# Copying the P V output banks out by ScalarE before VectorE normalises them, with smaller rings and a new order

## Chip, core and metric

The kernel runs on one core of a Trainium2 chip. The time is device microseconds for one execution, the median of several runs; a profiled execution of the same program gives the trace. TensorE (PE in the profile) does matmuls into PSUM, which has eight banks of 2 KB a partition. ScalarE (ACT) and VectorE (DVE) read the banks; GpSimd (POOL) and SyncE (SP) mostly issue transfers and pass on semaphores here.

## The reference

The input x has 2048 tokens of width 448, in bf16. It is normalised over the width, and two branches read the result xn:

```
xn = layernorm(x)
q, k, v = split(xn @ wqkv)                     # 16 heads of 28
logits[s, w] = q[s] . k[s - 2 w] / sqrt(28)    # w = 0..7, positions below 0 masked
s = concat_heads(softmax(logits) @ v) @ wo     # sliding, dilated attention
g = silu(gelu(xn @ w1 + b1) @ w2 + b2)         # 448 -> 1792 -> 448
out = x + s * g
```

## The kernel before

Tokens are reordered into the even and the odd ones, so that the dilation of 2 becomes a window of 8 neighbours. There are 16 tiles of 128 tokens and four chunks of 512. For each tile the kernel computes statistics (stats, L444), the normed row xn (norm, L479), a transpose of it (by TensorE for the first four tiles, by a DMA transpose for the others, dma_T, L398), the q and k rows (qk_rows, L576; matmuls L582), transposed by DMA into qkT, and the v rows (vproj, L599; matmuls L605), stored to v_hbm and loaded again in the layout of the blocks (values, L617).

Attention runs over nine blocks of 228 tokens (224 for the fifth). For a block, spread (L632) prepares the keys, scores_of (matmuls L757) fills four banks with scores, weights_of applies the exponential on ScalarE (L766) and the mask on VectorE (L772), and values_of (matmuls L786) multiplies the weights P with the values V into two banks. P V is done for two blocks together (four banks) and for block 8 alone. In output_of, VectorE normalises each bank in four steps: a 32x32 block transpose that brings the row sums into reach (L795), a reciprocal (L799), a transpose that spreads it back (L804), and a multiply into oT (L809), after which the bank is free.

The MLP runs by chunk: ff1 (matmuls L658, gelu on ScalarE L662), ff2 (matmuls L690, and L712 for the last two tiles), the gate (L724, L736, L740, or L731 for the last four tiles), and final with wo (matmuls L856, and L864 for the last two tiles), the gated sum (L876, L878, L883) and the output's transfer (L887).

Most matmuls use 64 of the 128 rows, two at a time: pair (L521) runs two jobs a and b with the first half of the rows for one and the second half for the other, and then swaps them. Between the halves a no-operation on GpSimd (L538) waits for the first half's matmuls and releases the second half's, the hop.

The order is made by a planner when the program is built (_Plan, L56): every piece of work is a task with an engine, a cost, its dependences, a priority, and the buffers it takes and gives. The planner takes the task that can start first, and among those that can start about then the one with the highest priority (tables PRIO and LATER, with corrections for single tasks by number in NUDGE). Each engine then runs its list in that order. Buffers come from rings: p_E (exponentials, four a block), p_v (values, one a block), p_xn (normed rows), p_b (the eight banks).

Of the kernel before, what the change touches and what calls it, by code (L numbers as in the profile page):

```python
# [8 lines left out]
F32 = mybir.dt.float32  # L9
BF16 = mybir.dt.bfloat16  # L10
ALU = mybir.AluOpType
ACT = mybir.ActivationFunctionType
# [5 lines left out]
TILED = 30  # L18
BURST = 3.5
NUDGE = {  # L20
    51: -17, 100: 72, 158: 186, 160: 19, 169: -108, 170: 110, 184: -158, 227: -173, 230: -199, 398: -138,
    428: -8, 461: 105, 892: 15,
}
LAST = 352
SAME = 20
# [155 lines left out]
def kernel(  # L181
# [12 lines left out]
    nc = tc.nc  # L194
    P = 128
    S, D, H, DH, F = A_x.shape[1], 448, 16, 28, 1792
# [14 lines left out]
    NW, NK, BACK, PAD = 57, 64, 7, 16  # L211
    VIS = []
    for v in range(9):
        n = NW - 1 if v == 4 else NW
# [18 lines left out]
    def sb(name, shape, dt=BF16):  # L233
        return const.tile(shape, dt, name=name)
# [29 lines left out]
    def ring(name, n, shape, dt=BF16, fifo=False):  # L264
        return _Pool([sb(f"{name}{i}", shape, dt) for i in range(n)], fifo)

    p_xn = ring("xn", 4, [P, 512])
    p_st = ring("st", 4, [P, 6], F32)
    p_E = ring("E", 15, [P, 8 * NW], fifo=True)
    p_dt = ring("dt", 2, [P, 512], F32)  # L270
    p_rd = ring("rd", 2, [P, H], F32)
    p_y = ring("y", 2, [P, D], F32)
    p_t = ring("t", 2, [P, D], F32)
# [4 lines left out]
    late_g = [w_in[:, kt, w * D:(w + 1) * D] for kt in range(3) for w in range(3)]  # L278
    p_g.bufs = p_g.bufs + late_g
    p_h = ring("h", 28, [P, CH], fifo=True)  # L280
    p_v = ring("v", 4, [P, 4, H // 2, 32], fifo=True)
    p_k = ring("kd", 2, [P, G, 4, 2 * NK], fifo=True)
    qk_tok = [sb(f"qk_tok{i}", [P, 2, H, 32]) for i in range(4)]
    p_f = _Pool([None])
# [1 line left out]
    p_b = _Pool([psum.tile([P, 512], F32, name=f"bank{i}") for i in range(8)])  # L286


    PRIO = {
        "project": (136, 119.5, 53, -443.5,),  # L290
        "project2": (38, -0, -278, -679.5,),
        "values": (-43, -278, -332, -863,),
        "attn": (95, 33.5, 174.5, 3, 187.5, 61, 136.5, 427, 178.5,),
        "ff1": (110.5, 186, 49, 159, -18.5, 129.5, 87, 189.5, 92, 142, 185, 18, 156, 198, 89, 31.5,
            202.5, 86, 62.5, -70.5, 140, 20.5, 76.5, 126.5, -3, 181, 92, 212.5,),
        "gelu": (120.5, -49.5, 86, -3,),
        "ff2": (195, -34.5, -231.5, 114.5, 68.5, 89, 111.5, 135, 195, 180.5, 162, 104, 430, 131,
            99.5, 28.5,),
        "final": (128.5, 2, 1, -16.5, 41.5, -2, 41, 203, 110, 65.5, 194.5, 162.5, 189.5, 134, 208,
            148,),  # L300
        "norm": (131, 11, 219.5, 294, 32, 66.5, 83.5, 207.5, 87.5, 115, 14, 127, 142.5, 64, 52.5,
            80,),
        "loads": (125, 117.5, -97.5, 131, 140.5, 12.5, 4, 84,),
        "stats": (49, 32, 205.5, 205.5, 131.5, 117, 41, 114, 130, 91, 157, 32.5, 140.5, 101.5,
            153.5, 258.5,),
        "turn_x": (198, 4.5, 200, 12.5, 258.5, 205.5, 24.5, 200, 24.5, -25.5, 154, 60, 132, 183.5,
            146.5, 78.5,),
        "turn_qk": (187, 122.5, 29, 78, -20.5, -22.5, 153.5, -151, 65.5, 6.5, 138, 32, 198.5, 162,
            35, 226.5,),
        "move_v": (146, 183, -68, 180, 92.5, 154.5, 241.5, 140.5, 190,),  # L310
        "store_v": (175, 54, 86, -1.5, 139.5, 189.5, -0, 18.5, 82.5, 213, 109.5, -126, 116, 13,
            53.5, 32,),
        "spread": (92, 81.5, 89, 141, 58, 25.5, 142, 46.5, 42,),
        "copies": (187, 4, 219, 15.5, 90, 177, 88.5, 31, 29, 20.5, 182, 51, 204.5, 49.5, 24,),
    }
    LATER = {"swap": 231.5, "qk": 165, "v": 171.5, "gelu": 94, "exp": 96.5, "mask": -4417.5, "pv": 209.5, "recip": 201.5, "os": 234, "y": 195, "tanh": 106, "g": 185.5, "sg": 100.5, "o": 89.5}

    plan = _Plan()

    def buf(pool, owner, i=0):  # L320
        return pool.bufs[owner.slots[pool][i]]

    def pe(n, k=1):
        return k * (n / 2400.0 + 0.0025)

    def act(n):
        return 0.15 + n / 1130.0

    def dve(n, r=1):
        return 0.15 + n / (960.0 * r)  # L330
# [186 lines left out]
    def behind(later, earlier):  # L517
        tc.add_manual_dep(later.ins, earlier.ins.name,
                          mybir.DependencyInfo(mybir.DependencyClass.Sync, mybir.DependencyReason.DATA), reason="row tiles")

    def pair(a, b, prio, early=False, before=(range(4),), after=(range(3),), late=((),), give=()):  # L521
# [21 lines left out]
        for i, ks in enumerate(after):  # L543
            def f3(k, ks=ks, n=n, i=i):
                p, q = buf(p_b, t, 0), buf(p_b, t, 1)
                for x in together([part(b, q, kt, 0, n + m) for m, kt in enumerate(ks)], [part(a, p, kt, 1, n + m) for m, kt in enumerate(ks)])[0]:
                    if not i:
                        behind(x, held["told"])
            u = plan.add("PE", pe(a.n, len(ks)), f3, [u if i else told], prio + LATER["swap"], give=give if i + 1 == len(after) else (), tail=0.15, mode=64)
            n += len(ks)  # L550
# [25 lines left out]
    def qk_rows(t, which, prio):  # L576
# [7 lines left out]
        def evac(a, own, i):  # L584
            b = qk_tok[t % len(qk_tok)]

            def fn(k):
                copy(k.on, b[:, which, :, :DH], buf(p_b, own, i)[:, :D].rearrange("p (h c) -> p h c", h=H))
            t_row[t].append(plan.add(("ACT", "DVE"), (act(D), dve(D)), fn, [a, t_qz[t % len(qk_tok)], t_qk.get(t - len(qk_tok))],
                                     prio + LATER["qk"], give=((p_b, own, i),)))  # L590
            if len(t_row[t]) == 2:
# [60 lines left out]
    def ff1(c, mt, prio, gate):  # L652
# [7 lines left out]
        def evac(a, own, i):  # L660
            def fn(k):
                nc.scalar.activation(buf(p_h, own, i)[:], buf(p_b, own, i)[:], ACT.Gelu_apprx_tanh,  # L662
                                     bias=b1[:, mt:mt + 1])
            t_h[(c, mt)] = plan.add("ACT", 0.69, fn, [a, t_b1] + gate, prio + LATER["gelu"],
                                    give=((p_b, own, i),), table=("gelu",))
# [53 lines left out]
    def gate(t, cs, n, a, own, i, biased, prio):  # L719
        if biased:  # L720
            y, pool, at, held = own, p_b, i, ((p_b, own, i),)
        else:
            def f2(k):
                nc.vector.tensor_tensor(out=buf(p_y, k)[:, :n], in0=buf(p_b, own, i)[:, :n], in1=b2[:, cs], op=ALU.add)  # L724
            y, pool, at = plan.add("DVE", dve(n), f2, [a, t_b2], prio + LATER["y"], take=(p_y,), give=((p_b, own, i),)), p_y, 0
            held = ((p_y, y, 0),)
        after = [a, y]

        if t >= NT - TPC:
            def f5(k):  # L730
                nc.scalar.activation(buf(p_g, k)[:, :n], buf(pool, y, at)[:, :n], ACT.Silu)  # L731
            t_g[t].append(plan.add("ACT", act(n), f5, after, prio + LATER["tanh"], take=(p_g,), give=held, table=("silu",)))
            return
# [56 lines left out]
    def output_of(b, po, i, a, prio):  # L790
        q, n1 = VIS[b]
        n, m = 8 * n1, -(-8 * n1 // 32)

        def f5(k):
            nc.vector.transpose(buf(p_dt, k)[:, :32 * m], buf(p_b, po, i)[:, :32 * m])  # L795
        d = plan.add("DVE", dve(32 * m), f5, [po], prio + LATER["recip"], take=(p_dt,))

        def f6(k):
            nc.vector.reciprocal(buf(p_rd, k)[:, :m],  # L799
                                 buf(p_dt, d)[:, :32 * m].rearrange("p (b c) -> p b c", c=32)[:, :, DH])  # L800
        r = plan.add("DVE", 0.25, f6, [d], prio + LATER["recip"] + 5, take=(p_rd,))

        def f7(_):
            nc.vector.transpose(buf(p_dt, d)[:, :32 * m].rearrange("p (b c) -> p b c", c=32),  # L804
                                buf(p_rd, r)[:, :m].unsqueeze(2).to_broadcast((P, m, 32)))
        rb = plan.add("DVE", dve(32 * m), f7, [r], prio + LATER["recip"] + 10, give=((p_rd, r, 0),))

        def f8(_):
            nc.vector.tensor_tensor(out=oT[:, a::2, q:q + 4 * n1],  # L809
                                    in0=buf(p_b, po, i)[:, :n].rearrange("p (l q) -> p l q", l=2),  # L810
                                    in1=buf(p_dt, d)[:, :n].rearrange("p (l q) -> p l q", l=2), op=ALU.mult)
        o = plan.add("DVE", dve(n), f8, [rb], prio + LATER["os"], give=((p_b, po, i), (p_dt, d, 0)))
        for t in range(q // P, (q + 4 * n1 - 1) // P + 1):
            t_oT[t].append(o)

# [144 lines left out]
    def f_b1(k):  # L960
# [3 lines left out]
                    give=((p_b, b1_at, 0),))  # L964
# [84 lines left out]
```

## Time and profile before

| | |
|---|---|
| median of 3 runs | 154.95 us (154.22 to 155.2) |
| profiled execution, its time | 154.93 us |
| its span | 153.2 us |
| busy: TensorE, VectorE, ScalarE, GpSimd | 146.5, 116.9, 91.5, 20.0 us |
| granted TensorE clock | 1.00 |

The span is the time from the first to the last instruction that the profile shows; the execution's own time has some 1.7 us more around it. In the chain of work that ended last, each row is followed back to what released it, so that time on the chain is time that the end hangs on. "bank" is a PSUM bank, "xT" holds the transposed normed rows and later, under the name oT, the attention output; "POOLq" and "SPq" are the instruction queues of GpSimd and SyncE; a line number such as L658 is a line of the kernel before.

### The profile page before, as it was taken

The numbers are of one execution on the slowest core, as the hardware profiler recorded it, in microseconds if no ns is written. First come the engines' busy times: TensorE is split into PE (matmuls) and PEld (weight loads), VectorE is DVE, ScalarE is ACT, GpSimd is POOL, SyncE is SP. The second block draws the span as 40 slices with busy tenths as digits, with TensorE's granted clock in tenths as the row PEclk, the third lists the DMA queues.
The fourth block names the chain that finished last, engine by engine and source line by source line (L and its number), as shares of the span: only waits on it lengthen the run. The fifth ranks groups of instructions, "written<-read, shape, count | busy, mean of one in ns | idle before, by whom it ended". The sixth has DMA issues, their size and how long they took to land.

```text
span 153.2 us, 5216 instructions
## 1 busy us (share of the span) xinstructions
PE 146.5 (96%) x2169; PEld 82.8 (54%) x2169; DVE 116.9 (76%) x285; ACT 91.5 (60%) x159; POOL 20.0 (13%) x53
## 2 busy tenths in 40 slices
PE   7799999999999999999999979999999999999990
PEld 2454444544455556455576733454569985754460
DVE  3887950573668857996898899789998966999962
ACT  3246887557695534574689578816984666660220
POOL 6536440110660000000130000000000000000000
PEclk9999999999999999999999999999999999999999
DMA  4999969999575361271389999722010030000131
GB/s 147 309 288 327 157 119 193 282 348 241 134 173 108 68 137 23 54 137 37 132 189 225 210 159 138 202 85 73 0 53 11 4 120 6 0 4 0 35 121 30
DMA packets 38022, 19.47 MB, mean 127 GB/s; under 512 B 24887, under 2 KB 37246, under 8 KB 37998
## 3 DMA queue, kind: packets, MB, share of 16 engines
q1 hardware_dynamic: 37246, 17.58, 51.0%
q0 software_dynamic: 608, 1.44, 3.6%
q8 instruction: 17, 0.28, 0.7%
q10 hardware_dynamic: 144, 0.11, 0.2%
q14 instruction: 7, 0.06, 0.1%
HBM read 9.42 MB, written 3.94 MB: 87 GB/s over the span
## 4 chain that ended last, share of the span: by engine, by line
PE 93%; DMA 2%; DVE 2%; issue 1%; ACT 0%; POOLq 0%
PE bank L658 28%; PE bank L690 24%; PE bank L582 14%; PE bank L605 7%; PE bank L856 7%; PE bank L786 4%; PE bank L712 4%; PE bank L757 3%; DMA x_sb<-in_A_x_dram 2%; PE bank L864 1%; DVE st L446 1%; PE bank L500 1%; DVE xn L481 0%; DVE xT L336 0%; DVE sg L876 0%
## 5 line engine op out<-in xcount | busy, mean ns | idle before, releaser
L658 PE MATMUL bank<-xT,w 64*128 64x512 bf16 x392 | 44.9, 376 | 1.3 <-POOLq L538 1.0
L662 ACT ACTIVATE h<-bank,b 128x512 bf16<-128x512 f32 x56 | 34.3, 686 | 17.5 <-PE bank L658 17.5
L690 PE MATMUL bank<-w,h 64*128 64x448 bf16 x392 | 39.8, 349 | 0.0
L658 PEld LDWEIGHTS <-w 64*128 64x128 bf16 x392 | 21.7, 94 | 22.0 <-POOLq L538 2.4
L690 PEld LDWEIGHTS <-h 64*128 64x128 bf16 x392 | 20.5, 94 | 15.7 <-issue 0.3
L582 PE MATMUL bank<-w_in,xT 64*128 64x448 bf16 (+1 forms) x212 | 24.7, 349 | 0.2 <-issue 0.2
L766 ACT ACTIVATE E<-bank 128x456 bf16<-128x456 f32 (+1 forms) x36 | 17.0, 557 | 4.8 <-PE bank L757 3.6
L334 ACT CAST qk_tok<-bank 128x448 bf16<-128x448 f32 x21 | 10.8, 535 | 12.8 <-PE bank L582 9.9
L582 PEld LDWEIGHTS <-xT 64*128 64x128 bf16 (+1 forms) x212 | 11.1, 94 | 9.4 <-POOLq L538 0.6
L795 DVE STREAM_TRANSPOSE dt<-bank 128x480 f32<-128x480 f32 (+1 forms) x18 | 12.1, 671 | 3.0 <-PE bank L786 2.9
L605 PE MATMUL bank<-w_in,xT 64*128 64x448 bf16 (+1 forms) x106 | 13.8, 350 | 0.1
L336 DVE CAST qk_tok<-bank 128x448 bf16<-128x448 f32 x11 | 6.7, 624 | 8.9 <-PE bank L582 8.8
L804 DVE STREAM_TRANSPOSE dt<-rd 128x480 f32<-128x480 f32 (+1 forms) x18 | 12.1, 675 | 0.6
L856 PE MATMUL bank<-wo,xT 64*128 64x448 bf16 x112 | 12.3, 349 | 0.0
L809 DVE TENSOR_TENSOR xT<-bank,dt 128x456 bf16<-128x456 f32 (+1 forms) x18 | 11.4, 632 | 0.6
L724 DVE TENSOR_TENSOR y<-bank,b 128x448 f32<-128x448 f32 x15 | 8.7, 618 | 4.1 <-PE bank L690 4.1
L446 DVE BATCH_NORM_STATS2 st<-x_sb 128x6 f32<-128x448 bf16 x16 | 9.6, 607 | 2.6 <-DMA x_sb<-in_A_x_dram 2.6
L772 DVE TENSOR_TENSOR E<-E,m_gen 128x456 bf16<-128x456 bf16 (+1 forms) x32 | 11.2, 390 | 0.0
L481 DVE TENSOR_SCALAR xn<-x_sb,mv,rstd 128x448 bf16<-128x448 bf16 x16 | 6.3, 401 | 4.4 <-POOL rstd L469 4.3
L736 ACT ACTIVATE t<-y 128x448 f32<-128x448 f32 x12 | 6.6, 583 | 4.0 <-DVE y L724 4.0
L856 PEld LDWEIGHTS <-xT 64*128 64x128 bf16 x112 | 6.6, 94 | 4.0 <-issue 0.4
L605 PEld LDWEIGHTS <-xT 64*128 64x128 bf16 (+1 forms) x106 | 5.9, 94 | 4.3 <-DVE xT L336 0.3
(74 smaller groups left out, 136.8 us busy)
## 6 DMA issues: line engine op xcount, KB each, us to landing
v<-v_hbm SPq DMA_DIRECT2D x14, 128.0 KB, 3.1
out_dram<-o SPq DMA_DIRECT2D x15, 112.0 KB, 1.7
v_hbm<-v_tok SPq DMA_DIRECT2D x13, 128.0 KB, 3.2
w<-in_B_w_dram SPq DMA_DIRECT2D x2, 672.0 KB, 7.4
w_in<-in_A_wqkv_dram SPq DMA_DIRECT2D x3, 336.0 KB, 4.4
w<-in_B_w_dram SPq DMA_DIRECT2D x2, 448.0 KB, 5.7
x_sb<-in_A_x_dram SPq DMA_DIRECT2D x4, 224.0 KB, 5.5
w<-in_B_w_dram SPq DMA_DIRECT2D x2, 336.0 KB, 6.3
```

The source lines that it names most:

```text
L446: nc.vector.bn_stats(out=buf(p_st, k)[:], in_=x_sb[:, t, :])
L582: return nc.tensor.matmul(ps[:, :D], xnT[r, kt, cs], w, start=start, stop=stop)
L605: return nc.tensor.matmul(ps[:, :D], xnT[r, kt, k0:k0 + P], w, start=start, stop=stop)
L658: return nc.tensor.matmul(ps[:], w1[r, kt, ms], xnT[r, kt, cs], start=start, stop=stop)
L662: nc.scalar.activation(buf(p_h, own, i)[:], buf(p_b, own, i)[:], ACT.Gelu_apprx_tanh, bias=b1[:, mt:mt + 1])
L690: return nc.tensor.matmul(ps[:, :D], buf(*h_at[(c, mt)])[r, cs], w2[r, mt, :], start=start, stop=stop)
L766: nc.scalar.activation(buf(p_E, k)[:, :8 * n], buf(p_b, a, at + i)[:, :8 * n], ACT.Exp, scale=SCALE)
L772: nc.vector.tensor_tensor(out=E, in0=E, in1=m[:, :, :, :n].rearrange("p i g q -> p (i g) q"), op=ALU.mult)
L795: nc.vector.transpose(buf(p_dt, k)[:, :32 * m], buf(p_b, po, i)[:, :32 * m])
L804: nc.vector.transpose(buf(p_dt, d)[:, :32 * m].rearrange("p (b c) -> p b c", c=32), buf(p_rd, r)[:, :m].unsqueeze(2).to_broadcast((P, m, 32)))
L809: nc.vector.tensor_tensor(out=oT[:, a::2, q:q + 4 * n1], in0=buf(p_b, po, i)[:, :n].rearrange("p (l q) -> p l q", l=2), in1=buf(p_dt, d)[: ...
L856: return nc.tensor.matmul(ps[:, :D], oT[r, kt, t * P:(t + 1) * P], wo[r, kt, :], start=start, stop=stop)
```

## The change

A ScalarE copy takes each output bank of P V into one of three fp32 buffers (p_oc); the bank is free after the copy. VectorE's first transpose and its last multiply read that buffer, which is free after the multiply. To make room, the ring of exponentials goes from 15 to 12 buffers, that of values from 4 to 3 and that of normed rows from 4 to 3. All priorities and the corrections by task number are other values, so that the order on every engine is another one; the number of matmuls of each kind is the same. The first P V stands nearer to the scores before it, and the parts of the projections of chunks 2 and 3 lie between other matmuls than before.

```diff
 NUDGE = {
-    51: -17, 100: 72, 158: 186, 160: 19, 169: -108, 170: 110, 184: -158, 227: -173, 230: -199, 398: -138,
-    428: -8, 461: 105, 892: 15,
+    51: -28, 142: -36, 144: -45, 161: 138, 169: -235, 185: 225, 391: -47, 400: -83, 471: 73, 656: -13,
 }
...
-    p_xn = ring("xn", 4, [P, 512])
+    p_xn = ring("xn", 3, [P, 512])
     p_st = ring("st", 4, [P, 6], F32)
-    p_E = ring("E", 15, [P, 8 * NW], fifo=True)
+    p_E = ring("E", 12, [P, 8 * NW], fifo=True)
     p_dt = ring("dt", 2, [P, 512], F32)
+    p_oc = ring("oc", 3, [P, 480], F32)
...
-    p_v = ring("v", 4, [P, 4, H // 2, 32], fifo=True)
+    p_v = ring("v", 3, [P, 4, H // 2, 32], fifo=True)
...
     PRIO = {
-        "project": (136, 119.5, 53, -443.5,),
+        "project": (202, 69.5, 85, -856.5,),
...
-    LATER = {"swap": 231.5, "qk": 165, "v": 171.5, "gelu": 94, "exp": 96.5, "mask": -4417.5, "pv": 209.5, "recip": 201.5, "os": 234, "y": 195, "tanh": 106, "g": 185.5, "sg": 100.5, "o": 89.5}
+    LATER = {"oc": 118.5, "swap": 56.5, "qk": 71.5, "v": 12.5, "gelu": 162.5, "exp": 120.5, "mask": -4534.5, "pv": 89.5, "recip": -32.5, "os": 165.5, "y": 165.5, "tanh": 184, "g": 198, "sg": 156, "o": 126}
...
         q, n1 = VIS[b]
         n, m = 8 * n1, -(-8 * n1 // 32)
 
+        def f4(k):
+            nc.scalar.copy(buf(p_oc, k)[:, :32 * m], buf(p_b, po, i)[:, :32 * m])
+        oc = plan.add("ACT", act(32 * m), f4, [po], prio + LATER["oc"], take=(p_oc,), give=((p_b, po, i),))
+
         def f5(k):
-            nc.vector.transpose(buf(p_dt, k)[:, :32 * m], buf(p_b, po, i)[:, :32 * m])
-        d = plan.add("DVE", dve(32 * m), f5, [po], prio + LATER["recip"], take=(p_dt,))
+            nc.vector.transpose(buf(p_dt, k)[:, :32 * m], buf(p_oc, oc)[:, :32 * m])
+        d = plan.add("DVE", dve(32 * m), f5, [oc], prio + LATER["recip"], take=(p_dt,))
...
         def f8(_):
             nc.vector.tensor_tensor(out=oT[:, a::2, q:q + 4 * n1],
-                                    in0=buf(p_b, po, i)[:, :n].rearrange("p (l q) -> p l q", l=2),
+                                    in0=buf(p_oc, oc)[:, :n].rearrange("p (l q) -> p l q", l=2),
                                     in1=buf(p_dt, d)[:, :n].rearrange("p (l q) -> p l q", l=2), op=ALU.mult)
-        o = plan.add("DVE", dve(n), f8, [rb], prio + LATER["os"], give=((p_b, po, i), (p_dt, d, 0)))
+        o = plan.add("DVE", dve(n), f8, [rb], prio + LATER["os"], give=((p_oc, oc, 0), (p_dt, d, 0)))
```

More of the change, by code (lines that the diff above doesn't have):

```diff
@@ L289 @@
     PRIO = {
-        "project": (136, 119.5, 53, -443.5,),
[L291 to L313, printed above, removed]
+        "project": (202, 69.5, 85, -856.5,),
+        "project2": (114, -190, -594.5, -809.5,),
+        "values": (0, -564, 74, -727.5,),
@@ new lines @@
+        "attn": (164, 121, 205.5, 195.5, -37.5, 94.5, 105.5, 136.5, 49.5,),
+        "ff1": (151, 64, 188.5, 155.5, 177, 3, 59, 130, 56, -20.5, -12, 167.5, 40, 92.5, 100.5,
+            218, 87, 232.5, -14.5, 15.5, 182.5, -4, 153, 44.5, 110, 100, 150.5, 99,),
+        "gelu": (5, 215.5, 67.5, 12.5,),
+        "ff2": (185, -34.5, 152, 114.5, -158, 89, -204, 135, 11, 180.5, 125, 104, 126, 131, 81.5,
+            16,),
+        "final": (114.5, 2, 60.5, -16.5, 81.5, -2, 184.5, 203, 40.5, 65.5, 54.5, 162.5, 82, 134,
+            205.5, -4,),
@@ new lines @@
+        "norm": (131, 11, 219.5, 294, 179.5, 63, 118.5, 52.5, 25, 317.5, 178.5, -11.5, 144.5, 86.5,
+            96, 179,),
+        "loads": (160.5, 228.5, -49.5, 138.5, -23, 89, -152.5, 235,),
+        "stats": (49, 32, 205.5, 205.5, 54, 194.5, 228.5, -10, 18.5, 52.5, -0, 66.5, 219.5, 81,
+            205.5, 33,),
+        "turn_x": (198, 4.5, 200, 12.5, 176, 139, 186, 191, 151.5, 5, 168.5, 178, 112.5, 54.5, 79,
+            -4,),
+        "turn_qk": (111.5, 183, 105.5, 54.5, 29, 52.5, 151.5, 25, 35.5, 156, 186.5, 158, 25, 115,
+            114.5, 8.5,),
@@ L314 @@
+        "move_v": (161, -9, 132.5, -7.5, -3.5, 69.5, -12.5, 148.5, 79,),
+        "store_v": (159.5, 24.5, 89, 3.5, 7, 80.5, 158, 192, 83, 45.5, 310, 255.5, 205, 19, 173.5,
+            -31.5,),
+        "spread": (113.5, 56, -14.5, -33.5, -37.5, 175.5, 170, -18.5, -26,),
         "copies": (187, 4, 219, 15.5, 90, 177, 88.5, 31, 29, 20.5, 182, 51, 204.5, 49.5, 24,),
     }
-    LATER = {"swap": 231.5, "qk": 165, "v": 171.5, "gelu": 94, "exp": 96.5, "mask": -4417.5, "pv": 209.5, "recip": 201.5, "os": 234, "y": 195, "tanh": 106, "g": 185.5, "sg": 100.5, "o": 89.5}
+    LATER = {"oc": 118.5, "swap": 56.5, "qk": 71.5, "v": 12.5, "gelu": 162.5, "exp": 120.5, "mask": -4534.5, "pv": 89.5, "recip": -32.5, "os": 165.5, "y": 165.5, "tanh": 184, "g": 198, "sg": 156, "o": 126}
```

## The prediction

> **What bounds the kernel now.** I read the totals first, then the chain of work that ended last, to learn which engine the end hangs on.
>
> ```profile
> span 153.2 us, 5216 instructions
> PE 146.5 (96%) x2169; PEld 82.8 (54%) x2169; DVE 116.9 (76%) x285; ACT 91.5 (60%) x159; POOL 20.0 (13%) x53
> PE 93%; DMA 2%; DVE 2%; issue 1%; ACT 0%; POOLq 0%
> ```
>
> TensorE (PE) carries 93% of the chain; VectorE (DVE) and ScalarE (ACT) count only where they make it stop. No matmul is added or removed, so the change can win only what TensorE loses between its matmuls. I therefore went through the chain in order of time (start, length, work) for stretches that are longer than their matmuls.
>
> ```profile
> 88.90 1.11 PE bank L658 x8
> ...
> 90.03 0.03 POOLq L538
> 90.06 0.94 issue
> 91.00 1.70 PE bank L658 x14
> ...
> 92.72 0.03 POOLq L538
> ...
> 92.79 4.71 PE bank L658 x42
> ...
> 98.26 0.65 PE bank L658 x6
> ...
> 103.25 1.64 PE bank L658 x14
> ...
> 104.91 0.03 POOLq L538
> ...
> 104.98 0.82 PE bank L658 x6
> ...
> 128.31 0.99 PE bank L658 x8
> ...
> 129.32 0.03 POOLq L538
> ...
> 129.40 3.92 PE bank L658 x34
> ```
>
> The row at 98.26 gives the clean rate: 0.65 / 6 = 0.108 us a matmul. From 88.90 to 97.50 (92.79 + 4.71) TensorE does 8 + 14 + 42 = 64 matmuls, worth 6.91, in 8.60: 1.69 lost, 0.94 of it one issue wait. From 103.25 to 105.80, 20 matmuls worth 2.16 take 2.55: 0.39 lost. From 128.31 to 133.32, 42 worth 4.54 take 5.01: 0.47 lost. Together that is 2.55 us, each time around a POOLq row: a pair of matmul groups swaps its row halves (pair, L521), and its second half stands behind a GpSimd hop (L538). The hop shows only where a second half directly follows its own first half; elsewhere another pair lies between, for which banks must be free. Where the banks were, the order of time by engine shows:
>
> ```profile
> 86.85 1.37 PE L786 MATMUL bank<-E,v 64*32 64x57 bf16 x128
> 87.61 0.68 DVE L795 STREAM_TRANSPOSE dt<-bank 128x480 f32<-128x480 f32 x1 [0.28 <-PE bank L786]
> 89.88 0.67 DVE L795 STREAM_TRANSPOSE dt<-bank 128x480 f32<-128x480 f32 x1
> 96.09 0.63 DVE L809 TENSOR_TENSOR xT<-bank,dt 128x456 bf16<-128x456 f32 x1
> ```
>
> P V (L786) fills four of the eight PSUM banks. VectorE normalises them one after another, 89.88 - 87.61 = 2.27 us each, and gives back the fourth at 96.72, 8.5 us after P V ended at 88.22.
>
> **The change, part by part.** *The copies.* 18 ScalarE copies to fp32, sixteen of 128x480 and two of 128x448, come in. The trace has no fp32 copy out of a bank; these groups (busy, mean ns) are nearest:
>
> ```profile
> L334 ACT CAST qk_tok<-bank 128x448 bf16<-128x448 f32 x21 | 10.8, 535 | 12.8 <-PE bank L582 9.9 <-issue 1.9 <-ACT E L766 0.7
> L736 ACT ACTIVATE t<-y 128x448 f32<-128x448 f32 x12 | 6.6, 583 | 4.0 <-DVE y L724 4.0
> L795 DVE STREAM_TRANSPOSE dt<-bank 128x480 f32<-128x480 f32 x16 | 10.8, 675 | 3.0 <-PE bank L786 2.9
> L804 DVE STREAM_TRANSPOSE dt<-rd 128x480 f32<-128x480 f32 x16 | 10.9, 679 | 0.6
> L809 DVE TENSOR_TENSOR xT<-bank,dt 128x456 bf16<-128x456 f32 x16 | 10.1, 633 | 0.6
> L740 DVE SCALAR_TENSOR_TENSOR g<-t,y 128x448 bf16<-128x448 f32 x6 | 3.6, 621 | 0.1
> ```
>
> Bounds 535 and 583 ns; I take 0.56, between them, since the first reads a bank as the copy does and the second writes fp32 as it does. 18 x 0.56 = 10.1 us (9.6 to 10.5) bring ScalarE from 91.5 to about 101. The other evacuations move between ScalarE and VectorE only by ones and twos. Where ScalarE has room this costs nothing; if it has none, each copy is 0.56 us on the path (thin places, below).
>
> *VectorE's reads.* Its first transpose and its multiply now read SBUF. L804 reads SBUF and takes 679 ns against 675 from a bank; L740 with both inputs in SBUF takes 621 for 448 elements against 633 for 456. I count 0. The Trainium skill (VectorE: DVE Perf Modes, "The TRN2 errata") prices an instruction at 58 cycles plus its elements from SBUF and at 120 plus its elements from PSUM, at 0.96 GHz; by that 36 instructions would each be 65 ns shorter, an estimated 2.3 us off VectorE, and the thin places below would hold, giving 153.3 us. The trace does not agree: 679 stands against 675.
>
> *The banks.* Three are free after three copies, some 1.7 us after P V instead of about 2.3, 4.5 and 6.8; the fourth copy needs one of the three buffers back from a normalisation, so about 3.5 us instead of 8.5. The new order uses it: in TensorE's new instruction list no second half directly follows its own first half (four did). The 2.55 us should then go, save that nothing ties the 0.94 of issue to the hop. I take 2.55 - 0.94 = 1.61 and keep 2.55 as the other end.
>
> *Fewer buffers.* Twelve exponentials are three blocks; in the new order no more than three blocks of scores stand before a P V that frees some (blocks 2, 3, 4, then P V of 2 and 3), so the ring holds. With three value buffers, block 3's load may start after the first P V and has over 20 us to land. With three xn buffers, tile 7's norm waits for tile 4's transpose, where VectorE has idle time. All these: 0; if such a cover fails, TensorE stands for as long as the load or the row is late.
>
> *SP's queue.* Two loads of w2 now stand behind the V store of tile 2 and a key transpose.
>
> ```profile
> 31.68 5.54 SPq L400 DMA_TRANSPOSE qkT<-qk_tok  x2
> w<-in_B_w_dram SPq DMA_DIRECT2D x2, 448.0 KB, 5.7
> ```
>
> Tile 2's V cast now follows the gelus of chunk 0, at about 27 us by my count; with 5.54 / 2 = 2.8 us for the transpose and the issues between, w2 goes out by about 33 and lands 5.7 later, by 39, against a first use near 42. That is 3 us of cover; beyond it, each us late is a us.
>
> *Thin places.* P V now stands nearer to its scores, and the normalisations nearer to their users. I summed the work between four pairs of points in the new order, from the rows above and these:
>
> ```profile
> 126.49 2.42 ACT L662 ACTIVATE h<-bank,b 128x512 bf16<-128x512 f32 x4 [0.60 <-PE bank L658]
> 108.70 1.88 ACT L766 ACTIVATE E<-bank 128x456 bf16<-128x456 f32 x4 [0.29 <-PE bank L757]
> 114.07 1.30 DVE L772 TENSOR_TENSOR E<-E,m_gen 128x456 bf16<-128x456 bf16 x4
> 121.58 0.69 DVE L883 TENSOR_TENSOR o<-x_sb,sg 128x448 bf16<-128x448 bf16 x2
> 141.33 1.15 DVE L724 TENSOR_TENSOR y<-bank,b 128x448 f32<-128x448 f32 x2
> 30.06 9.93 PE bank L658 x92
> 136.13 1.32 PE bank L690 x14
> 138.21 2.65 PE bank L690 x28
> 140.86 0.76 PE bank L856 x8
> 141.62 1.43 PE bank L712 x7
> ...
> 145.34 0.76 PE bank L864 x4
> 140.78 0.63 DVE L809 TENSOR_TENSOR xT<-bank,dt 128x456 bf16<-128x456 f32 x1
> ```
>
> 1. From the scores of block 1 to P V of blocks 0 and 1 TensorE has L690 x28 and eight of L582, 2.65 + 0.76 = 3.4 us; the last mask needs four exponentials and itself, 0.2 + 1.88 + 0.4 = 2.5. Slack 0.9.
> 2. From P V of 4 and 5 to the second half of the next L690 pair: L658 x34 (3.67), x14 (1.32), L856 (0.76), 5.75 us. ScalarE has three copies in their runs (about 0.5 each) and six gelus at 2.42 / 4 = 0.61: 5.2. Slack 0.5.
> 3. From P V of 6 and 7 to P V of 8: 0.76 + 9.93 + 0.76 + 0.65 + 1.32 = 13.4 us. VectorE waits for the first 0.76 and a hop, then has two gated sums (like the 1.15 row), two o (0.69), four normalisations (9.08) and three masks (1.0): 12.8. Slack 0.6.
> 4. From P V of 8 to the last products (L864): 1.32 + 0.76 + 2.65 + 0.76 + 1.43 + 0.76 + 1.43 = 9.1 us. VectorE takes two y after the 2.65 run (at 4.73), then the second normalisation: 4.73 + 0.15 + 1.15 + 2.27 = 8.3. Slack 0.8, where the kernel now has 145.34 - 141.41 = 3.9.
>
> TensorE runs its list in order, so at each place anything beyond the slack stops all matmuls behind. Each sum may be off by half a us either way, so the four lose 0 to about 1.5 us together; I take 0.3, near the low end, since all slacks come out positive.
>
> *The sum.* -1.61 + 0.3 = -1.3. The profiled execution took 154.93 us, 1.73 of it outside its span, which stays: 153.6, with 151.9 of span. It stands 0.02 below the median of the runs, 154.95, so nothing is shifted.
>
> **The rivals.** *A, the forecast:* hops gone, thin places hold; 153.6, by its bounds 152.4 (2.55 won, none lost) to 154.8 (1.61 won, 1.5 lost).
>
> *B, no gain:* the hops go and as much returns at the four places, 0.4 each: 154.9. For it: all slacks are under 1 us. Against: ScalarE and VectorE keep to these durations almost to the hundredth in the rows above.
>
> *C, slower: the fourth copy blocks ScalarE.* With three buffers it waits for a normalisation, and the exponentials, gelus and casts listed behind it on ScalarE wait too. It decides once VectorE, busy elsewhere when P V ends, starts normalising later than the slack, some 0.7 us. Then three of the four double P V lose one normalisation less the slack, 2.27 - 0.7 = 1.6 each, 4.7 together: 154.93 - 1.61 + 4.7 = 158.0; with one such place, 154.9. For it: VectorE is 76% busy and has casts, masks and sums ahead of the normalisations. Against: the new order puts other work ahead of most fourth copies.
>
> *D, more:* the issue wait belonged to the hop and goes too, and nothing is lost: 154.93 - 2.55 = 152.4. For it: it stands right at the swap. Against: the other three swaps have none.
>
> **How the numbers follow.** A 0.40, B 0.18, C 0.28, D 0.14. About 1% (1.5 us) is what a measurement of this kernel tells from no change: faster is below 153.4, slower above 156.5. A lies about evenly around 153.4: faster 0.14 + 0.18 = 0.32, same 0.22 + 0.18 = 0.40, slower 0.28. The range goes from 152.0, just below D, to 157.8, most of the way to C; A's own range is 152.4 to 154.8.
>
> **What would show it.** Right: no POOLq row of L538 in the MLP stretches of the new chain, L658 x6 at 0.65 throughout, ScalarE near 101 us with copies near 560 ns, VectorE's busy time within 1 us of 116.9, P V banks rewritten within 4 us. Wrong: matmul rows released by ScalarE (copy, gelu or mask behind it) with waits over 0.5 us, above all ahead of P V of 4 and 5, P V of 8, or L864; matmuls waiting for w2 at the first L690; transposes from SBUF clearly under 650 ns.

## The result and the profile after

| | before | changed |
|---|---|---|
| median, first comparison | 154.76 us | 152.62 us (152.38 to 153.2) |
| ratio, 95% interval | | 0.987 (0.983 to 0.991) |
| median, second comparison, another chip | 154.86 us | 152.45 us (152.39 to 152.52) |
| ratio, 95% interval | | 0.984 (0.982 to 0.986) |
| profiled execution | 154.93 us | 152.38 us |

The changed kernel is 2.1 to 2.4 us faster. From L799 on, its lines are numbered up to four higher: the copy is L795, the normalisation L799, L803, L808 and L813, the products with wo L860 and L868. The totals and the chain by engine:

```profile
span 150.7 us, 5223 instructions
PE 145.4 (97%) x2169; PEld 77.3 (51%) x2169; DVE 116.6 (77%) x284; ACT 99.4 (66%) x178; POOL 19.7 (13%) x53
PE 94%; DMA 2%; DVE 2%; issue 0%; ACT 0%
```

The span is 2.5 us shorter, and POOLq, the sign of the hop, has left the chain. TensorE's waits (line, releaser, total, times, longest) are two, both at the start of the kernel; none is for w2 or for a load of values:

```profile
PE bank L500 <- DVE xn L481: 0.9, 1, 0.9
PE bank L349 <- PEq L1037: 0.8, 1, 0.8
```

The chain in order of time, at the stretches where the kernel before lost its 2.55 us, and at its last matmuls:

```profile
90.55 6.04 PE bank L658 x56
...
100.18 3.78 PE bank L658 x34
...
120.19 9.93 PE bank L658 x92
...
130.88 0.65 PE bank L658 x6
...
146.42 0.61 PE bank L712 x14
```

56 matmuls in 6.04 us, 92 in 9.93 and 6 in 0.65 are the clean 0.108 us each; 34 in 3.78, right behind a P V, are 0.1 over it. TensorE ends at 146.42 + 0.61 = 147.03. The same row of the kernel before:

```profile
148.97 0.61 PE bank L712 x14
```

It ends at 149.58. The difference is 2.55 us. That this is also the prediction's sum for the swaps is partly chance. In both kernels the matmuls right behind a P V take 0.1 us longer, and two of the prediction's stretches, at 103.25 and at 128.31, begin behind a P V: 0.2 of its 2.55 has not left. P V itself takes 0.16 longer in the changed kernel. On the other side, a stop of the kernel before that the prediction does not list has left:

```profile
62.11 0.20 issue
62.32 0.74 PE bank L582 x6
```

"issue" is a wait for nothing that the profile shows, and six such matmuls take 0.57 elsewhere: 0.37 us together. A second trace of the kernel before (below) has 0.43 there; neither trace of the changed kernel has such a stop. It is no direct swap, for six other matmuls lie between the halves, though the profile names a hop for the weight load there (PEld):

```profile
PEld L582 <- POOLq L538: 0.6, 1, 0.6
```

What held it stays open.

The banks after P V of blocks 2 and 3, in the order of time by engine:

```profile
80.12 1.40 PE L786 MATMUL bank<-E,v 64*32 64x57 bf16 x128
80.88 1.48 ACT L795 COPY oc<-bank 128x480 f32<-128x480 f32 x3
...
84.64 0.58 ACT L795 COPY oc<-bank 128x480 f32<-128x480 f32 x1
...
90.75 0.64 DVE L813 TENSOR_TENSOR xT<-oc,dt 128x456 bf16<-128x456 f32 x1
```

P V ends at 81.52. Three banks are free at 82.36, 0.84 us later, the fourth at 85.22, 3.7 us later. VectorE finishes the fourth normalisation only at 91.39, 9.9 us after P V: if it still read the banks, the fourth would be held until then. The first experiment tests what that would cost.

### The profile page after: what moved, and what is told of

It is laid out like the page before. It is cut to its first block, busy times and chain, and to the rows that moved or that the text cites. A ratio compares the mean times of both kernels' runs of the same rounds, so it can differ in the third digit from the quotient of the medians.

```text
span 150.7 us, 5223 instructions
## 1 busy us (share of the span) xinstructions
PE 145.4 (97%) x2169; PEld 77.3 (51%) x2169; DVE 116.6 (77%) x284; ACT 99.4 (66%) x178; POOL 19.7 (13%) x53
## 4 chain that ended last, share of the span: by engine, by line
PE 94%; DMA 2%; DVE 2%; issue 0%; ACT 0%
PE bank L658 28%; PE bank L690 25%; PE bank L582 14%; PE bank L860 7%; PE bank L605 7%; PE bank L786 4%; PE bank L712 4%; PE bank L757 3%; DMA x_sb<-in_A_x_dram 2%; PE bank L868 1%; DVE st L446 1%; PE bank L500 1%; DVE xn L481 0%; DVE xT L336 0%; DVE sg L880 0%
## 5 line engine op out<-in xcount | busy, mean ns | idle before, releaser
L658 PE MATMUL bank<-xT,w 64*128 64x512 bf16 x392 | 44.1, 376 | 0.0
L662 ACT ACTIVATE h<-bank,b 128x512 bf16<-128x512 f32 x56 | 34.2, 688 | 10.3 <-PE bank L658 10.1
L690 PE MATMUL bank<-w,h 64*128 64x448 bf16 x392 | 40.3, 349 | 0.0
L658 PEld LDWEIGHTS <-w 64*128 64x128 bf16 x392 | 20.4, 94 | 21.3
L690 PEld LDWEIGHTS <-h 64*128 64x128 bf16 x392 | 18.5, 94 | 16.7
L582 PEld LDWEIGHTS <-xT 64*128 64x128 bf16 (+1 forms) x212 | 10.8, 94 | 10.3 <-issue 0.5
L799 DVE STREAM_TRANSPOSE dt<-oc 128x480 f32<-128x480 f32 (+1 forms) x18 | 12.0, 668 | 2.3 <-ACT oc L795 2.2
L860 PE MATMUL bank<-wo,xT 64*128 64x448 bf16 x112 | 13.7, 349 | 0.0
L605 PE MATMUL bank<-w_in,xT 64*128 64x448 bf16 (+1 forms) x106 | 13.7, 350 | 0.0
L808 DVE STREAM_TRANSPOSE dt<-rd 128x480 f32<-128x480 f32 (+1 forms) x18 | 12.1, 675 | 0.6
L813 DVE TENSOR_TENSOR xT<-oc,dt 128x456 bf16<-128x456 f32 (+1 forms) x18 | 11.4, 632 | 0.6
L795 ACT COPY oc<-bank 128x480 f32<-128x480 f32 (+1 forms) x18 | 9.2, 560 | 2.1 <-PE bank L786 1.3
L334 ACT CAST v_tok<-bank 128x448 bf16<-128x448 f32 x12 | 6.1, 532 | 4.3 <-PE bank L605 2.7
L860 PEld LDWEIGHTS <-xT 64*128 64x128 bf16 x112 | 5.9, 94 | 4.8 <-issue 0.6
```

Of the source, the lines that this page charges most:

```text
L334: nc.scalar.copy(o, i)
L582: return nc.tensor.matmul(ps[:, :D], xnT[r, kt, cs], w, start=start, stop=stop)
L605: return nc.tensor.matmul(ps[:, :D], xnT[r, kt, k0:k0 + P], w, start=start, stop=stop)
L658: return nc.tensor.matmul(ps[:], w1[r, kt, ms], xnT[r, kt, cs], start=start, stop=stop)
L690: return nc.tensor.matmul(ps[:, :D], buf(*h_at[(c, mt)])[r, cs], w2[r, mt, :], start=start, stop=stop)
L799: nc.vector.transpose(buf(p_dt, k)[:, :32 * m], buf(p_oc, oc)[:, :32 * m])
```

## The experiments

To hold an order fixed while one part changes, each engine was given its list of tasks from one of the two kernels (ORDER), and took them in that order only. "Direct swaps" are second halves that directly follow their own first half.

**The order alone.** The changed kernel's lists on every engine, with its small rings, but without the copies: a task without work stands in the place of each, and VectorE reads the banks as before.

```diff
+ORDER = {"PE": (...), "DVE": (...), "ACT": (...), ...}   # the changed kernel's lists
-        oc = plan.add("ACT", act(32 * m), f4, [po], ..., take=(p_oc,), give=((p_b, po, i),))
+        oc = plan.add("CLK", 0.0, None, [po], 300)
...
-        o = plan.add("DVE", dve(n), f8, [rb], ..., give=((p_oc, oc, 0), (p_dt, d, 0)))
+        o = plan.add("DVE", dve(n), f8, [rb], ..., give=((p_b, po, i), (p_dt, d, 0)))
```

> The changed kernel's order on every engine, instruction for instruction, with its small rings, but without the 18 copies: VectorE normalises straight out of the banks again. Theory 'banks' (the order gains only because ScalarE gives the P V banks back early): TensorE must now wait where the order rewrites banks that VectorE still holds (2.27, 4.5, 6.8 and 9.1 us after P V), at four double P V's; I work out 0.5 to 1.5 us at each, so 2 to 5 us more than the changed kernel's 152.6: about 155.5, at or above the kernel before, with TensorE rows that wait for L809's bank. Rival 'order' (the new priorities alone, whatever the banks): 152.6 within 0.5, or a little less, since ScalarE has 9.2 us less to do.

Measured: 161.9 us, ratio to the kernel before 1.050 (1.047 to 1.052), 9.3 us above the changed kernel. The sign is that of the theory of the banks, the size about twice the most that I expected. Its chain, where the first double P V's banks are wanted by the scores of the next block (L763):

```profile
67.15 0.64 DVE xT L817
...
67.84 0.37 PE bank L763 x15
68.21 2.14 PE bank L696 x14
70.35 1.12 PE bank L611 x6
71.47 1.64 PE bank L696 x14
73.11 0.76 PE bank L864 x8
```

The same matmuls on the changed kernel's chain (two lines with L690 for L696, L605 for L611 and L860 for L864):

```profile
65.34 1.32 PE bank L690 x14
66.67 0.57 PE bank L605 x6
67.24 1.32 PE bank L690 x14
68.56 0.76 PE bank L860 x8
```

The scores wait for the last multiply of the fourth normalisation (L817); the first matmul behind them starts 68.21 - 65.34 = 2.87 us later than in the changed kernel. By the products with wo the lag is 73.11 - 68.56 = 4.55: another 1.68 us is lost in matmuls that merely take longer, 2.14 against 1.32, 1.12 against 0.57. Why, the stretches of one microsecond show (stretch, its length, busy time of PE, PEld, DVE, ACT and POOL with their counts, then the granted clock, the DMA share and GB/s):

```profile
66.00:67.00 1.00, 0.00 (x0) 0.00 (x0) 0.93 (x3) 0.14 (x1) 0.00 (x0) 1.00 0.22 47
...
68.00:69.00 1.00, 1.00 (x23) 0.51 (x18) 0.00 (x0) 0.76 (x2) 0.00 (x0) 0.79 0.00 0
...
70.00:71.00 1.00, 1.00 (x8) 0.44 (x6) 0.54 (x1) 0.00 (x0) 0.00 (x0) 0.50 0.00 0
```

After the stop the clock is granted at half for over 3 us: these stretches, and the ones between that are left out, put it from about 68.6 to 71.9. A wait for a bank is thus paid nearly twice here. The other 4.4 of the 8.9 us by which TensorE ends later come behind: another 1.5 at the P V of blocks 2 and 3, the rest at gelus and gated sums that VectorE and ScalarE do late.

**The copies alone.** The lists of the kernel before, with the copies put into ScalarE's where they could start first; two fp32 buffers, since three don't fit beside the large ring of exponentials, and rings of three for values and normed rows.

```diff
+ORDER = {"PE": (...), "DVE": (...), "ACT": (...), ...}   # the lists of the kernel before
-    p_E = ring("E", 12, [P, 8 * NW], fifo=True)
+    p_E = ring("E", 15, [P, 8 * NW], fifo=True)
-    p_oc = ring("oc", 3, [P, 480], F32)
+    p_oc = ring("oc", 2, [P, 480], F32)
```

> The kernel before, its order on every engine instruction for instruction, with the 18 ScalarE copies put into ScalarE's list where they can start first, into two fp32 buffers (three do not fit beside the 15 buffers of exponentials that this order needs), and value and normed-row rings of three. Theory 'banks through order': the four direct swaps are in the list and stay, so nothing is gained: 154.8 within 0.5, the POOLq rows of L538 still on the chain. Rival 'copies alone': 152.6, the rows gone. Rival 'ScalarE blocked' (my C: with a small ring the later copies wait in ScalarE's list for a normalisation and hold the gelus and exponentials behind them): 156 to 158, with TensorE waiting for gelus or exponentials behind a copy.

Measured: 162.05 us, 1.051 (1.047 to 1.055), above all three expectations; the sign is that of ScalarE blocked. Its waits:

```profile
DVE dt L811 <- ACT oc L807: 13.0, 4, 4.9
ACT oc L807 <- DVE xT L825: 5.2, 6, 1.7
PE bank L872 <- DVE xT L825: 3.7, 2, 3.2
PE bank L670 <- POOLq L550: 1.0, 1, 1.0
```

VectorE stands 13.0 us for copies that stand behind other work on ScalarE, copies stand 5.2 us for a buffer that VectorE has not given back, and the hops (L550) are still there, since the order of the matmuls has not moved. Behind the stop of 3.2 us, which ends at 104.38, the clock is at half until about 107.6. Neither part alone brings a gain; the place of the copies in ScalarE's list and the two buffers are mine, so this prices this version of "copies alone", not every one.

**Six direct swaps put back.** The changed kernel, with one dependence that makes each pair of chunk 3's ff1 wait for the one before, so that six second halves follow their own first halves.

```diff
+                if c == 3 and i:
+                    hs[i].deps.append(ff1_last[c])
```

> The changed kernel with one dependence added: in the MLP of chunk 3 a pair starts only when the pair before it has ended, so that six pairs of L658 swap directly in a row; the rest of TensorE's list up to there is unchanged. It measures a direct swap by itself. Theory of the sum: 1.61 / 4 = 0.40 us each, six cost 2.4: about 155.0, six POOLq rows of L538 in that stretch. Rival 'the issue wait belongs to the hop': 2.55 / 4 = 0.64 each, 3.8: 156.4, with issue waits of up to 0.9 in some of the six. Rival 'only the visible gap': 0.1 each, 153.2.

Measured: 154.67 us, 1.001 (0.999 to 1.003): the gain is gone. The chain of its profiled execution (154.51 us):

```profile
120.30 0.88 PE bank L658 x8
...
121.21 0.03 POOLq L538
...
121.28 1.70 PE bank L658 x14
...
124.88 1.68 PE bank L658 x14
```

With another 14 that are left out here these are 50 matmuls, worth 5.40 us; they take 6.26, 0.29 for each of three swaps. The profiled execution is 2.13 us above the changed kernel's, 0.36 a swap with what follows from it. So a direct swap costs 0.29 to 0.36 us, a little under the 0.40 expected, and none of the six drew a long issue wait.

**The kernel before, traced again.** No edit.

> The kernel before once more, unchanged, for a second trace. If the issue wait of 0.94 us at 90.06 belongs to the hop or to that place of the program, it stands there again, about as long, and the span is 153.2 within 0.3. If it is chance, it is gone or elsewhere, and the span is about 152.3 without it.

Measured: 154.34 us. Its chain at the first swap:

```profile
89.11 1.11 PE bank L658 x8
...
90.27 0.14 issue
90.41 1.70 PE bank L658 x14
...
92.20 4.71 PE bank L658 x42
```

The issue wait is 0.14 us where it was 0.94, and the stretch loses 0.89 instead of 1.69; the other two lose 0.39 and 0.46 as before. How long the wait is thus differs from one execution to another; but it stands behind the same hop both times, and behind the other three it is 0.05.

**The copies with the old priorities.** The changed code and rings, but the priorities of the kernel before, from which the planner makes an order of its own (892 is 910 with the copies counted).

```diff
-    51: -28, 142: -36, 144: -45, ...
+    51: -17, 100: 72, 158: 186, ..., 910: 15,
-    LATER = {"oc": 118.5, "swap": 56.5, "qk": 71.5, ...}
+    LATER = {"oc": 118.5, "swap": 231.5, "qk": 165, ...}
```

> The code of the changed kernel (copies, three buffers, small rings) with the priorities and single corrections of the kernel before; the planner makes a new order from them. In that order three second halves directly follow their first half (four before the change, none in the changed kernel). Theory 'banks through order': most of the gain needs an order that uses the free banks; three swaps at 0.34 (six cost 2.05 in the run before) put it at 153.7, and waits of an order that nobody has tuned come on top: 153.7 to 156. Rival 'copies are enough once the planner knows them': 152.6 within 0.5. Rival 'ScalarE blocked': over 157, with gelus or exponentials behind copies.

Measured: 155.53 us, 1.006 (1.003 to 1.009). Three direct swaps are left in its order, two of them on the chain of its trace, and TensorE waits 0.7 us for exponentials. Copies in an order that the planner makes around them lose only 1 us, but without the new priorities they gain nothing.

**Two buffers instead of three.** The changed kernel's lists and rings, but two fp32 buffers.

```diff
-    p_oc = ring("oc", 3, [P, 480], F32)
+    p_oc = ring("oc", 2, [P, 480], F32)
```

> The changed kernel's order on every engine, instruction for instruction, with two fp32 buffers instead of three: the third copy of a double P V waits for the first normalisation and the fourth for the second, and what stands behind them in ScalarE's list waits too. My rival C prices a normalisation that ScalarE must wait for at 2.27 us less a slack of 0.7, 1.6 at each of the four double P V's: up to 6.4 more, about 156 to 159. If the copies' waits are covered by banks and rings: 152.6 to 153.2.

Measured: 160.06 to 161.44 us in three executions and 163.42 in a fourth, 1.049 (1.040 to 1.058). The middle of the three, 161.13, is 8.5 us above the changed kernel, and all are above the 156 to 159 expected. The waits in the trace of the fastest:

```profile
ACT oc L802 <- DVE xT L820: 12.8, 5, 4.2
...
PE bank L697 <- ACT oc L802: 1.4, 1, 1.4
```

Copies stand 12.8 us for a buffer, and TensorE waits 1.4 and 0.9 us for two of them, besides 1.9 for a cast and 1.6 for a gelu that come late on ScalarE. This is rival C, one buffer away from the kernel that was measured.

**Every copy done twice.**

```diff
+            for _ in range(2):
                 nc.scalar.copy(buf(p_oc, k)[:, :32 * m], buf(p_b, po, i)[:, :32 * m])
```

> The changed kernel's order with every copy done twice (the same bank into the same buffer), 9.2 us more for ScalarE and up to 0.5 us more before each normalisation. By my slacks: place 2 (three copies ahead of the gelus of chunk 2, slack 0.5) loses about 1.0, place 3 (slack 0.6) nothing or little, place 4 (slack 0.8, one or two copies ahead) 0 to 0.2: about 153.8. If ScalarE has more room than I summed: 152.6 to 153.0. If copies lie on the path of TensorE: up to 9 us more, 161.

Measured: 154.12 us, 0.999 (0.996 to 1.002), 1.5 to 1.7 us above the changed kernel, for 18 more copies of 559 ns in the mean. That is about 0.09 us for each: most of ScalarE's added work is covered, but not all. The size is near the 153.8 expected, the place is not. TensorE ends 1.47 us after the changed kernel's; on the two chains 0.36 of that is lost by the first double P V, another 0.44 by the second, and only 0.16 at place 2, where about 1.0 was expected.

**The new priorities without copies.** The changed priorities and rings, no copies (edit as in the first experiment), and the planner free.

> The changed kernel's priorities and small rings without the copies, the planner free to make another order that fits the banks VectorE holds: three direct swaps in it, one of them of L690. It tells whether the 9.3 us that the same order lost without copies were the order's fault. Theory 'banks': a free planner avoids most of the waits but not all: 154.5 to 158, between the kernel before and the forced order at 161.9. Rival 'priorities alone': 152.6 to 153.6.

Measured: 162.96 us, 1.055 (1.050 to 1.060), a miss: the planner finds nothing better than the order that was forced in the first experiment. Its chain runs through four normalisations on end, from 131.73 to 140.85 us, though TensorE, which has other work there, waits only 0.2 us for the last of them; there are longer stops before that (the last section).

**The changed kernel, timed and traced again.** No edit.

> The changed kernel once more, unchanged, timed beside the kernel before on one chip, with a second trace. If the gain is what the traces say (about 1.74 us of direct swaps in both traces of the kernel before, nothing new lost), the ratio is 0.986 to 0.989, 152.4 to 152.8, and the chain again holds no POOLq row of L538. If the issue wait of the first trace of before was part of it, the ratio is nearer 0.983.

Measured: 152.45 us, 0.984 (0.982 to 0.986). The chain again has no hop of L538 in it. The ratio lies under the 0.986 to 0.989 expected, near the 0.983 named for the case that the issue wait of the kernel before is part of the gain.

**The order alone, with the large rings.** As the first experiment, with 15 exponentials, 4 value and 4 xn buffers.

> The run that had the changed kernel's order without copies (161.9), now with the rings of the kernel before: 15 buffers of exponentials, 4 of values, 4 of normed rows. My step 'fewer buffers: 0' says that the rings bind nothing in this order: 161.9 within 0.5. If the small rings cost something that the copies' gain had hidden, it is faster than that by what they cost, 1 us or more.

Measured: 161.93 us, 1.045 (1.041 to 1.048), beside 161.9 and 1.050 with the small rings. The smaller rings are not what costs those 9 us; by the ratios they cost some 0.7 us, by the medians nothing, and the intervals of the two ratios overlap.

## Why the prediction came out as it did

*The swaps.* The mechanism held: four direct swaps left the chain, and TensorE's end moved by about what they had cost. The term was 1.61 with 2.55 as its other end. Without the 0.2 that stays behind P V, and with 0.05 of issue at each hop, the four cost 1.46 us in the first trace of the kernel before and 1.45 in the second, 0.36 each, as the six that were put back. What the sum does not have is the stop at 62.11, 0.37 and 0.43 us. In the second trace TensorE ends at 148.99 (its last row on the chain is 0.61 from 148.38), 1.96 after the changed kernel's 147.03. So the measured 2.1 to 2.4 is about 1.5 of swaps, 0.4 of that stop and, in some executions of the kernel before, an issue wait of up to 0.9 on top. Leaving that wait out of the price of a hop was right: six swaps put back had none. Leaving it out of the gain was not: in both traces it stood behind a hop that is now gone, and it went with it.

*The thin places.* Here the sum was mis-sized: 0.3 lost was the estimate, and nothing was lost. The rows of the changed kernel, in the order of the four places:

```profile
52.45 1.78 DVE L772 TENSOR_TENSOR E<-E,m_gen 128x456 bf16<-128x456 bf16 x5
55.44 1.42 PE L786 MATMUL bank<-E,v 64*32 64x57 bf16 x128
...
103.35 2.42 ACT L662 ACTIVATE h<-bank,b 128x512 bf16<-128x512 f32 x4 [0.66 <-PE bank L658]
105.87 1.49 PE L690 MATMUL bank<-w,h 64*128 64x448 bf16 x14
...
130.93 1.00 DVE L772 TENSOR_TENSOR E<-E,m_gen 128x456 bf16<-128x456 bf16 x3
132.78 0.70 PE L786 MATMUL bank<-E,v 64*32 64x57 bf16 x64
...
141.13 0.64 DVE L813 TENSOR_TENSOR xT<-oc,dt 128x456 bf16<-128x456 f32 x1
142.63 0.92 PE L868 MATMUL bank<-wo,xT 128*128 128x448 bf16 x4
```

From the end of the first row of each pair to the start of its matmuls: 55.44 - 54.23 = 1.2 us, 105.87 - 105.77 = 0.1, 132.78 - 131.93 = 0.85, 142.63 - 141.77 = 0.9. Predicted were 0.9, 0.5, 0.6 and 0.8. Three sums were right to 0.3 us; at the second place the gelus came 0.4 us later than summed, and 0.1 us was left.

*The copies.* 560 ns each, as taken:

```profile
L799 DVE STREAM_TRANSPOSE dt<-oc 128x480 f32<-128x480 f32 x16 | 10.8, 672 | 2.3 <-ACT oc L795 2.2
L795 ACT COPY oc<-bank 128x480 f32<-128x480 f32 x16 | 8.3, 563 | 0.8 <-ACT h L662 0.8
```

ScalarE comes to 99.4 us, not 101: the copies add 9.3, not 10.1, because copies in a run overlap (three in 1.48 us), and one preparation of keys, 1.2 us, has moved to VectorE. At the four double P V's three banks are free after 1.1, 0.8, 2.5 and 1.3 us, mostly before the 1.7 of the sum, for the first copies start while P V still fills the other banks. The fourth is free after 4.5, 3.7, 6.0 and 5.6 us, against 3.5: later than summed, and the sign "rewritten within 4 us" came at most once. It is still earlier than the 8.5 of the kernel before, and TensorE waited for none of them.

*VectorE's reads.* No gain, as counted: 672 ns from SBUF against 675 from a bank, and the multiply 633 against 633. The Trainium skill (VectorE: DVE Perf Modes, "The TRN2 errata") would have made each an estimated 65 ns shorter; the trace does not agree.

*The rivals.* The time lies on D's 152.4, and from the first trace of the kernel before to the changed one D's account comes out: the long issue wait went, and nothing was lost. By how much is luck, for the next trace of the kernel before had 0.14 in place of 0.94; the forecast's own sum with nothing lost gives 153.3. B's losses at the thin places did not come. C did not come either: in the changed kernel no copy waits for VectorE; the copies' waits are 1.3 us for P V itself and 0.8 behind a gelu. With two buffers it came, and larger than priced. What I priced too low is how much hangs on the copies once the order counts on them: 2 to 5 us by the expectation, 9.3 measured, of which the clock alone is 1.7.

*Left open.* Why the free planner without copies did no better than the forced order was not taken apart further. Whether an order without copies that avoids just the four direct swaps would do as well wasn't tried, nor what holds TensorE in the issue waits. A fourth fp32 buffer does not fit beside the rings and wasn't tried.

## What to carry to other kernels

Where one engine carries nine tenths of the chain, look for the small fixed losses between its instructions (here some 0.36 us at each direct swap) and ask what resource would let other work stand between; here it was a PSUM bank some microseconds earlier. An early copy out of a bank and the order that uses it are worth something only together: either one, forced into a fixed order without the other, cost over 7 us, and copies with an order planned around them by the old priorities still lost 1. Size the ring of the copies so that the last one of a group does not wait for the slow reader; one buffer less turned a gain of 2 us into a loss of 7.

## What the runs showed of the hardware

A short stop of TensorE can cost more than itself. In the run of the order alone the longest wait was 2.3 us, and the clock was then granted at half from about 68.6 to 71.9 us, which cost another 1.68. The Trainium skill (TensorE: Matmul & The Clock Gate, "Why this matters for your kernels") advises no idle gaps over about 3 us between bursts of matmuls; the trace disagrees with that as a safe bound. The new priorities without copies show it with shorter stops still, the longest of these 0.73 us:

```profile
121.16 0.78 PE L756 MATMUL bank<-qkT,kd 64*128 64x57 bf16 x31 [0.40 <-ACT E L765]
122.67 0.79 PE L857 MATMUL bank<-wo,xT 64*128 64x448 bf16 x2 [0.73 <-ACT E L765]
124.16 0.74 PE L857 MATMUL bank<-wo,xT 64*128 64x448 bf16 x6 [0.70 <-DVE xT L810]
125.40 1.64 PE L857 MATMUL bank<-wo,xT 64*128 64x448 bf16 x8
```

Three stops within 3.5 us, 1.83 us together, and the last row's eight matmuls, 0.76 us at full clock, take 1.64. Not every such stop does it: in the profiled execution with two buffers TensorE waits up to 1.9 us at a time, and its mean clock is 0.999; the other three executions have 0.977 to 0.987. In the traces of the kernel before and of the changed one the mean clock is 0.997 to 1.0. The second surprise is the issue wait on TensorE's queue, 0.94 us in one execution of the kernel before and 0.14 at the same place in another.
